# All of PSUM in one tile: bank pairs for the scores of two engines, single banks for the rest, and 74 score blocks on VectorE

## The chip, the cores and the metric

The kernel runs on one core of one Trainium2 chip. The metric is the device time of one execution in microseconds (us), as the median of several runs. The profile is one further execution, recorded by the hardware; PE is TensorE, DVE VectorE, ACT ScalarE, POOL GpSimd, SP SyncE.

## The reference, cut to what matters

A token sequence of 2048 x 448 goes two ways, and a gate per token mixes the results. Way A is softmax attention with 16 heads of 28 columns and an output projection. Way B is a two-dimensional real FFT, a product with a filter, and the way back.

```python
g = sigmoid((x * gate_w).sum(-1, keepdims=True))
q, k, v = (x @ wqkv).reshape(B, S, 3, 16, 28)...
p = softmax(einsum("bhqd,bhkd->bhqk", q, k) * 28 ** -0.5)
a = einsum("bhqk,bhkd->bhqd", p, v) @ wo
y = irfft2(rfft2(B_x) * (w_r + 1j * w_i))
out = g * a + (1 - g) * y
```

Here x is the input A_x.

## The kernel before

**Attention.** The heads stand in four groups of four (index g), the queries in four columns of 512 (index c): 16 pairs (g, c), which `plan_steps` numbers n = 0 to 15. For each n there are 16 key tiles of 128 (index kt), so 256 blocks (n, kt) of four heads. A score matmul takes the 32 rows of one head (28 columns, padding, and two rows that carry norms) against 512 queries, so it fills one of four row tiles of PE, and four matmuls of four different heads can stand side by side.

The exponential is made by two engines. `ND` says how many key tiles of each n go to VectorE; the rest go to ScalarE.

- ScalarE: a step is two heads of one block. PE writes two score matmuls into the two banks of `psA` or `psB`, which alternate; one `activation` of 1024 columns (line 1034) writes two slots of `ring`. The two steps of a block take heads 0 and 1, then heads 2 and 3.
- VectorE: for each of the four heads of a block PE writes one score matmul into a single bank (`bgi`), and a `tensor_scalar` of 512 columns (line 993, "the clamp") adds a bias, clamps at zero and writes the result as a 16-bit integer whose bits are a bfloat16: a piecewise linear power of two. GpSimd makes three further copies with shifted phase by `int64_add` (line 1003). So a block on VectorE has four versions of its probabilities, and each is multiplied with its own version of V (`vd`).

The product with V takes four column tiles (four heads) at a time and adds up in one bank of its own, `pv`: one set of four matmuls for a ScalarE block, four sets for a VectorE block. At the end of each n, `normalise` evacuates `pv`, and a chain of small transfers and two VectorE operations scales the result into `q`.

**Everything else.** `proj_group`, `w_block`, `v_block` and `x_block` make Q, K and V from x; `background` makes the FFT as matmuls with constant matrices in stages (`fwd`, `fwd2`, `mid`, `inv`); `out_tile` and `last_tile` add the output projection and the inverse transform for each 128 tokens. Each such product is an `Item` that occupies one single bank, of three (`bgt`), from its first matmul until VectorE or ScalarE has evacuated it.

**The order.** Every operation is registered with `Sched.op`, with the item whose bank it takes (`acq`) and the one that it gives back (`free`). Nothing decides at run time: `TABLE` holds two packed lists, the order in which all operations are issued and the bank of each item in the order of registration. `run` unpacks them and emits the operations; codes from `FILL0` up are groups of dummy matmuls on zeros into `pv`. The engines run their parts in that order and wait for one another by semaphores.

Of the kernel before, what the change touches and what calls it, by code (L numbers as in the profile page):

```python
# [15 lines left out]
F32 = mybir.dt.float32  # L16
U16 = mybir.dt.uint16
# [21 lines left out]
    "eNoN1mNjWEsUQNHxnMG5SW2ltm3bNtPUtm3btm3bto3UdvveX9hf1jakJbHEkXCCJDqJQWKSWCQ2iUPikngkPiEkAUlIEpHEJAkJI0lJMpKc"  # L39
    "UJKCZCApSU6SiniSmuQijHQlQAKiCScZSRoiSXaSlkQlitQk6Ugmkp7UILVINZKNZCG5SVUSheQhWUkOUodkJiVJKRKNlCa1SV5SloSQUFKO"  # L40
    "1Cf5SH5SgBQiBUkxUp6UIRVJYVKEFCXFySZSgWwmlUgJ0oq0JVvIVrKStCPbyHayiqwmVcgOsoZMJGtJZTKJTCZTyFSyjqwnG0g3YpVXG8l0"
    "MoPMJLOIU7PJHDKX7CTziCDzySy/gCwkcWk8Gp8uIovJDL+ELCUJaEK6jKDaRRLRnqQxWU5WkECFqMQ0Ck1Co9JoNDqNQcNoTBqLxqZx6G6y"
    "h+wl+0ioak6iqqfkGXlOXpCXJILcIQ3IfhJJ7pID5B55RV6TKOo+eUMekI7kIXlEHpNo6iCJrqaRGKouOUSS0mQ0pupEYqnkNAU9TJ6Qt2SD"
    "j63ekfckjvpA4qp4qhc5Qo6SlDS+akGOkan0I/lEptHPpAlJoBKq6fQLSaS+Qip6nCRWJ0hqmkR9gxk0TH0lp8hpkoau8WnpGXKWJFX1SG9y"
    "jpwnF8hMepEkU61JOnqJXCZXyFVyjSRX18kNcpOkULfIbZKeplRlaAaakZ4kmWhinoSnUj+hLE2t0qhYvByNzcvTXxCNz/XpVFpVgX6H6Dy9"
    "oqYiHUQyqIzqG0nGm5HvJAaPyX+Qn6Qp+UUyqT+QWf2DSjSLyqo6k+okDk/OK9OGpArtSDvRuDwhX+ezqc60C82uEvD1PhEP439IUp5D/SX/"
    "CKGUMrrac9qV5lSCSqqoprkU0Kw0G81Oc9DcKif9TXLR3NRQS/PQPCovzUdTcEfzKk/z05keaUDj83wqhBagmWlBWogWpkVofpWFhtJ4vCgt"
    "RtuTNqQ47U4LqIw8E+9BS9Ke1PJCyhhtHC+oCqv0vIjiJgMvTaUppoqqtLy4siYlr0p70RKqGi2pqtNSKh0vrVJzYXrTUlSZYaSMKkHT8Bq0"
    "Jk3FmSmrsvFyipi/UF5l5dn5SFpB5eGjaEU1mlZSeXkOPobWopVVB/IbqqiqKhcfS535AdVUTg6mNq2ucvMaqh7tQurTBjQfr0NrKm9qqc+u"
    "MC/DG9J4Bk1dWlsV4XVUDNOI1FUFeEJTkNdTCUwjmpnXV1l4WV6IJzHFeQlegefnFXkDFcs0VDFNXFOTN1KNVWNandfg8U0TVZQnMk1VMhOY"  # L50
    "YryZim1K8lo8jglXIaa5qsRb08o8mklpWqgIVY6X5m1oW9qOtlItVXnenjbjrVUqE86/uaimB2mjEpsmtK1KbkJNO1WVN6XNeQQPM9X4F9de"
    "NeFNeQeV0Xx3P9xP98t1VN1oJ1WX1+MZTDjtoprT7qSz+u0iaBTzx1XhLWhX1ZK2591UJlOKd1cduPQ9lPLpTHrTU/VSrWhtXoeDN9763iqN"
    "6aNa8+imr3I+tRlMve+n0po2vL8aQtE34o35ABX4gSqFSWoym0FqKB1GB6shqi3/6xrwf244JZ76+rwdH6oa8qKG+WGqI2/FC5jhqqDpxkeo"
    "fIb7Qkb4kWqU6sU78eKmO89jSpjRKovpzceoljyr6UvGqh68Jw/xXXkLXsaE+qG8GR2n8prxqjOP7xP4YTyhH8wnqES+iBnC4/i4PrGfqPrQ"
    "SWqyym860C58iipsipmpKokP81F9NN+HT1PZTHRf2cTw09UMNVP15aVNH5LT9KWzVAqf0s9Wa30qH9PH8rF9at+PpvFlzRy1kKb1i+hiOosu"
    "oXPVUprOD+fzVDkzgvfn5c18NYYvUHfoXXqPrqD36QO6ki5UI+gq+pA+oo/pE7qarqFP6SI1lq+l6+h6uoEO4BvpM7pYae/5JjqOL1HP6Qu6"
    "mb6kkXQ8f0WXqtd0C91Kt9FBdDtdpsbT5WoCXaFWquV0IK9kNvoddBwdSEuZQTypX6WS+Yl0El2tZvI1ajKdzquZmmatGs1n8XVqvZrEa5iS"
    "pqLZoPrxyXwG36jm8lF8Np9CJ/A5fCTfpPrTWmYi36yqmwF0Hp/Ct6gKpoqparapZXyrmk13qCW8tgk3c+g0nstsV03MPLpTNTUr+HKewyzl"
    "u1Qzs1vN5xFmj1rE1/LspoVZyTfyxXw+3ac6mTw+r9+rxpCFPJ9fx/P7TfyAmkv3qwK+oG9r2pmD6pA6rPbwOqa1mcqbm728kD+idvBMfifP"
    "7LP4oyqr38wHkGPqFF1AT9Mz9Cw9R7P54+o8vUCz+xz+Ir1EL9MTajW/Qrfwq3QVv0av0xv0pKprbtJTah9fw7uaBby/6WNu0dv0jFrPT6vc"  # L60
    "Zj9vY97QKL6zOad20rNqF91N99DzagPfS/fR/fQAPUgP0QtqFz9Md/Mj9Cg9Ri+q43QZPUFP8kuqgzlJT/GO5hzfzi+ro/wYv6KuqlZmG+9h"
    "eprz/Dg/wa+pLia9v64y+BvqMK9nuptDPLk/wluam+qWus/7mduqgq/oe5mG5gG/o7byC/wir+Qr+7uqij/IQ3goz+jbmwO8kbmnBphu5r6q"
    "6h+om7yaf6j6mt7mPb3C39K7fKCpbx6pW/yxOs3P8idqmhllnqqrfDi5xO/xZ2qcGW/e0RfquXrCL/OyfqIp55/ya3y0eakiVRPfwLxSTf0Y"
    "81rd5s38ZPNGhfs7/AV/q5r7l/ydivAzTDFf3JfwJX0p38K/V/PNB9WflPaRfJB5xT+qT2q2iefL+Bv8DL/OJ5np5rP6ogabIeQRf8af88J+"
    "gvmqvqnH/Av/yhubsaaIf8inmO/qh+JMsE/8p/qlPvOpRjLFNBtK3vJ3/D3/rf6omWaO+av+8n98sVloiP7AP/J/SorlZpYhYoihWgmm+5Hh"
    "huvXfK5ZYRaZN/w3L+qFpuIPlzqnz+V/8G+8oVda6wXmO8/th5lGfpmJKn5y0L+40UvMPPM/SMLqbn6p8drpaMIK1N39SpOE9fA9fS8PLLro"
    "7QO9yYSxpGyECdGhOoZIxvr47aaxj6qFiKKTMycOmW2Gieg6mtYiVHgRQ4OIIraY3SamiCVi6h1mp6nuY+lAxNYJxFGTUMTRIWK/SSJQ1PBx"
    "dZjYZ/aYeDq+TqDjiaEmvqjla/s6vq6v51eZ1SaRSCzq+7giqWjgy/uEerOZ7deYRHqUH+3H+LE+sR7nx/sJfq+ZQE6aOT6JDtNpxFbT0ifV"
    "yXRynVa08W19O9/exxEXTAff0Y80KXRKvc7U9J38QdPKf6Cp9Ef6iaYTqXUanVwcM+nFZ5pWp9OpRGyRXp8xJ8xh84WmFhl0Rl1I7DKFRV/f"
    "z6cQ030ykUmfNwdMZp1FZ9U5RUqRS3T2XXwGsdYcN9l0PnHKZNcD/EA/yGcU+cVgP8Tn0Dl1EXHEFBWnTSaRS2cVQ/1Zk1vHYHl0NnHOxGTD"  # L70
    "fD6dV180XX1mEYtlEbFZft3f3zIFdEEdh2UXf+h685fmEHlEIb3BFNYlxT9aStwx5UURTVgFQVleUVQ/N7lFaXHJFNNTfHE91d8zZcRDU0KX"
    "1DXEffPAlNI1RWldQBQU70w8VkaXFa19OXHbxGfFxHBfVidgI3xCVk1UFIlYdVFOV9Dl9RNTQnyjE/1I/9J8pxV1FVFJ/6A/aRU9yVfWTQVj"
    "03xV8Ys+Mq9NNV1c1Bdf6TNTVTcQv+ld89hU1zV0LVFbTPZPTU0dwmrpSiLSGNZMWPbFvDDzfG093y/wdfRCX1fU0+lZBpaRZWJ1tWOhLAqL"
    "yj6YuOyjWeQvm/o6GsvMGosGuol4axrphnoEaShasEainqgsWrJWrDVrwxKztqwda8+ysSO+sc7OOrAlfqPJwXKyXOyKaaKb6twsD8vLOrJO"
# [184 lines left out]
class Item:  # L259
    def __init__(self):  # L260
        self.bank = None
# [1209 lines left out]
```

## Time and profile before

| | |
|---|---|
| device time, median of 3 runs | 381.05 us (381.0 to 381.06) |
| device time of the profiled execution | 380.98 us |
| its span, first to last instruction | 379.2 us |
| busy time of PE | 371.3 us |
| busy time of ScalarE | 351.1 us |
| busy time of VectorE | 339.1 us |
| busy time of GpSimd | 234.4 us |
| granted clock of PE | 1.00 |

The profile page names for each group of instructions the line, the engine, the operation, the tiles written and read, the shape, the count, the busy time of the group, the mean duration of one, and the idle time of the engine ahead of them with its releaser. Almost all matmuls stand on line 432, the helper `mm`, so groups are told apart by their tiles: `psA` and `psB` are score pairs, `bg<-q,k` the scores for VectorE, `pvb` the products with V (from `ring` or from `pd`), other `bg` the remaining products. A matmul's recorded duration is longer than the time that it holds the engine up, since matmuls overlap; distances between starts say more. The timeline has one line for a run of like instructions: start, duration, engine, line, operation, tiles, shape, count. A row of the view by stretches gives the stretch, its length, then for each engine the busy time with the number of instructions, then the granted clock, the share of the DMA engines and the rate.

### The profile page before, as it was taken

Reading aid. Unit: us, or ns where it says so; the run is one execution under the profiler, and the core shown is the slowest. Engines: PE = TensorE matmul, PEld = TensorE weight load, DVE = VectorE, ACT = ScalarE, POOL = GpSimd, SP = SyncE. Lnnn points to the kernel's source line nnn. Section 1 sums busy time; section 2 is a strip of 40 time slices with the busy share of each in tenths; the row PEclk is TensorE's granted clock in tenths of the full one; section 3 lists DMA queues with packets and bytes.
Section 4 is the critical chain, followed back from the end, with each engine's and each line's share of the span. In section 5 each row is a group of like instructions: output and inputs, shape, how many; then the busy total and the mean of one; then the engine's idle time right before and its main releaser. Section 6 shows DMA issues by size and latency. Waiting matters only on the chain.

```text
span 379.2 us, 12643 instructions
## 1 busy us (share of the span) xinstructions
PE 371.3 (98%) x5117; PEld 142.4 (38%) x5117; DVE 339.1 (89%) x665; ACT 351.1 (93%) x389; POOL 234.4 (62%) x264
## 2 busy tenths in 40 slices
PE   8999999999999999999999999999999999999996
PEld 6634223342433333234333434233333323433564
DVE  1768899999999999999999999999999999988744
ACT  2799999999999999999999999999999999999841
POOL 4446465866778866565553565778597778483510
PEclk9999999999999999999999999999999999999999
DMA  6511101010210112211322212223222122222132
GB/s 145 157 34 44 29 18 36 4 36 2 41 52 22 44 41 54 55 38 30 68 60 93 69 40 49 57 61 70 45 64 74 30 69 72 86 64 72 35 103 75
DMA packets 31158, 21.23 MB, mean 56 GB/s; under 512 B 16260, under 2 KB 29052, under 8 KB 31100
## 3 DMA queue, kind: packets, MB, share of 16 engines
q1 hardware_dynamic: 29708, 19.96, 20.7%
q8 instruction: 40, 0.66, 0.7%
q10 hardware_dynamic: 1392, 0.46, 0.5%
q14 instruction: 18, 0.15, 0.1%
HBM read 14.51 MB, written 1.96 MB: 43 GB/s over the span
## 4 chain that ended last, share of the span: by engine, by line
PE 55%; ACT 31%; issue 6%; DVE 4%; DMA 2%; POOL 1%; SPq 0%; DVEq 0%; ACTq 0%; POOLq 0%
ACT ring L1034 31%; PE bg L432 24%; PE pvb L432 17%; PE psA L432 7%; PE psB L432 6%; DVE pd L993 2%; PE bg L435 1%; DMA CS<-cCS 1%; DVE X L1419 1%; POOL pd L1003 1%; DMA Wg<-in_B_w_i_dram 0%; DVE X L1298 0%; DVE q L1178 0%; DVE t L1362 0%; DVE wpq L1224 0%
## 5 line engine op out<-in xcount | busy, mean ns | idle before, releaser
L1003 POOL INT64_ADD pd<-pd x207 | 211.9, 1038 | 96.7 <-DVE pd L993 27.4
L1034 ACT ACTIVATE ring<-psA 128x1024 bf16<-128x1024 f32 x187 | 201.7, 1078 | 4.7 <-PE psA L432 3.2
L1034 ACT ACTIVATE ring<-psB 128x1024 bf16<-128x1024 f32 x187 | 201.7, 1079 | 2.6 <-PE psA L432 1.4
L993 DVE TENSOR_SCALAR pd<-bg 128x512 uint16<-128x512 f32 x276 | 180.9, 681 | 8.5 <-PE bg L432 3.5
L432 PE MATMUL pvb<-pd,vd 128*32 128x512 bf16 x1104 | 96.9, 384 | 0.1
L432 PE MATMUL bg<-q,k 32*128 32x512 bf16 x276 | 96.3, 383 | 0.2
L432 PEld LDWEIGHTS <-k 32*128 32x128 bf16 x1024 | 40.1, 91 | 122.4 <-issue 117.7
L432 PE MATMUL psB<-q,k 32*128 32x512 bf16 x374 | 73.2, 383 | 1.3 <-ACT ring L1034 0.7
L432 PE MATMUL psA<-q,k 32*128 32x512 bf16 x374 | 72.8, 383 | 0.5 <-ACT ring L1034 0.2
L432 PE MATMUL pvb<-ring,vw 128*32 128x512 bf16 x748 | 67.9, 384 | 0.0
L432 PEld LDWEIGHTS <-vd 128*32 128x32 bf16 x1104 | 25.3, 94 | 35.5 <-issue 31.1
L432 PEld LDWEIGHTS <-vw 128*32 128x32 bf16 x748 | 17.5, 94 | 22.7 <-issue 20.5
L432 PEld LDWEIGHTS <-xT 128*128 128x128 bf16 (+5 forms) x512 | 20.3, 97 | 10.7 <-issue 9.7
L432 PE MATMUL bg<-xT,wpq 128*32 128x512 bf16 (+3 forms) x244 | 21.2, 383 | 0.1
L1362 DVE TENSOR_TENSOR t<-bg,Wg 128x450 bf16<-128x450 f32 x32 | 18.8, 614 | 0.6 <-DMA Wg<-in_B_w_i_dram 0.4
L432 PE MATMUL bg<-xT,wpk 128*32 128x512 bf16 (+2 forms) x240 | 18.9, 383 | 0.0
L432 PE MATMUL bg<-wvr,xT 128*128 128x112 bf16 (+2 forms) x192 | 13.7, 213 | 0.0
L1178 DVE TENSOR_TENSOR q<-pvs,Rb 128x512 bf16<-128x512 f32 x15 | 10.9, 729 | 2.6 <-DMA Rb<-rsc 2.6
L1298 DVE TENSOR_TENSOR X<-bg,oc 128x226 bf16<-128x226 f32 (+1 forms) x32 | 12.3, 386 | 0.5
L432 PEld LDWEIGHTS <-CS 128*32 128x32 bf16 x384 | 9.0, 95 | 9.9 <-issue 5.6
L432 PE MATMUL bg<-xtok,CS 128*32 128x225 bf16 (+1 forms) x192 | 11.2, 294 | 0.7 <-DMA CS<-cCS 0.7
L742 DVE TENSOR_SCALAR k<-bg 128x512 bf16<-128x512 f32 x15 | 10.3, 685 | 1.3 <-PE bg L432 1.1
(117 smaller groups left out, 315.4 us busy)
## 6 DMA issues: line engine op xcount, KB each, us to landing
Rb<-rsc SPq DMA_DIRECT2D x60, 64.0 KB
CS<-cCS SPq DMA_DIRECT2D x16, 192.0 KB
V<-xtok SPq DMA_DIRECT2D x16, 113.0 KB
Wg<-in_B_w_i_dram SPq DMA_DIRECT2D x64, 28.1 KB
xtok<-Ab SPq DMA_DIRECT2D x16, 112.5 KB
xtok<-in_A_x_dram SPq DMA_DIRECT2D x3, 448.0 KB
Wg<-in_B_w_r_dram SPq DMA_DIRECT2D x32, 28.1 KB
out_dram<-wpq SPq DMA_DIRECT2D x6, 112.0 KB
```

What stands on the lines that cost most here:

```text
L432: self.pin(self.nc.tensor.matmul(out, lhsT=lhsT, rhs=rhs, start=start, stop=stop, **kw))
L435: self.pin(self.nc.tensor.transpose(out=out, in_=in_, identity=self.c("ident")[0:n, 0:n]))
L742: self.pin(nc.vector.tensor_scalar(out=dst, in0=self.bgi(it), scalar1=SQ, scalar2=None, op0=ALU.mult))
L993: self.pin(nc.vector.tensor_scalar(out=ys[:, s, :].bitcast(U16), in0=self.bgi(it), scalar1=127 * UNITS, scalar2=0.0, op0=ALU.add, op1=ALU. ...
L1003: self.pin(nc.gpsimd.int64_add(out=fl(pds), in0=fl(ys), in1=PHASE[f] * 0x0001000100010001))
L1034: self.pin(nc.scalar.activation(out=self.ring[:, u0:u0 + len(st), :], in_=slot[:, 0:len(st), :], func=ACT.Exp, scale=LN2 / UNITS))
L1178: e = self.dve(dv(512), lambda: self.pin(nc.vector.tensor_tensor(out=dst, in0=pvs[:], in1=self.Rb[:], op=ALU.mult)), ds, kk, lk=True)
L1298: self.pin(nc.vector.tensor_tensor(out=free_dims(self.X1[:, t, :], [[F, 2], [-1 if dif else 1, n]], (F - 1) * dif), in0=free_dims(self.bgi ...
L1362: self.pin(nc.vector.tensor_tensor(out=out[:], in0=self.bgi(it)[:, 0:F2].rearrange("p (a f) -> p a f", a=2), in1=free_dims(Wg[:], [[F, 2], ...
L1419: self.pin(nc.vector.tensor_tensor(out=free_dims(self.zt[0:FN], [[128, 4], [1, 128]], 512 * t), in0=self.bgi(it)[0:FN, :].rearrange("p (a ...
```

## The change

PSUM becomes one tile of eight banks, `banks`. Bank 7 is `pv`. An item gets a mask of bank kinds: 15 for a single bank, 7 for a pair (`slot`, two neighbouring banks). ScalarE's steps and VectorE's blocks both take pairs: a block has two operations on PE of two heads each, and two clamps of 1024 columns, in place of four of each with 512. All other products take single banks. The steps no longer have a fixed slot or a wait for the exponential two steps before; they acquire and free a pair like any item. `ND` goes from a sum of 69 to 74. The order and the banks are new lists; the old order holds six groups of dummy matmuls, the new one none. In the prologue and in `last_tile` the fixed homes in `psA` and `psB` become items. `kr[0] += self.ktr` adds a wait to the later reuse of `k[0]`.

```diff
 class Item:
-    def __init__(self):
-        self.bank = None
+    def __init__(self, mask=15):
+        self.bank, self.mask = None, mask
...
-    ND = [2,4,5,5]+[5,5,4,4]+[4,4,5,5]+[5,5,4,3]
+    ND = [3,5,5,5]+[5,5,4,4]+[4,4,5,5]+[5,5,5,5]
...
-        self.psA = ps.tile([P, 2, 512], F32, name="psA")
-        self.psB = ps.tile([P, 2, 512], F32, name="psB")
-        self.pv = ps.tile([P, 512], F32, name="pvb")
-        self.bgt = [ps.tile([P, 512], F32, name=f"bg{i}") for i in range(3)]
+        self.banks = ps.tile([P, 8, 512], F32, name="psA")
+        self.pv = self.banks[:, 7, :]
...
+    def slot(self, item):
+        return self.banks[:, item.bank:item.bank + 2, :]
+
     def bgi(self, item, dt=F32):
-        t = self.bgt[item.bank][:]
+        t = self.banks[:, item.bank, :]
...
-            for s in range(4):
-                it = Item()
-
-                def fm(s=s, g=g, c=c, kt=kt, it=it):
-                    self.mm(self.bgi(it), self.k[g][32 * s:32 * s + 32, 128 * kt:128 * kt + 128],
-                            self.q[g][32 * s:32 * s + 32, 512 * c:512 * c + 512], True, True, tile_position=(32 * s, 0))
+            for h in (0, 2):
+                it = Item(7)
+
+                def fm(h=h, g=g, c=c, kt=kt, it=it):
+                    for s in (h, h + 1):
+                        self.mm(self.slot(it)[:, s - h, :], self.k[g][32 * s:32 * s + 32, 128 * kt:128 * kt + 128],
+                                self.q[g][32 * s:32 * s + 32, 512 * c:512 * c + 512], True, True, tile_position=(32 * s, 0))
...
-                    self.pin(nc.vector.tensor_scalar(out=ys[:, s, :].bitcast(U16), in0=self.bgi(it),
+                    self.pin(nc.vector.tensor_scalar(out=ys[:, h:h + 2, :].bitcast(U16), in0=self.slot(it),
                                                      scalar1=127 * UNITS, scalar2=0.0, op0=ALU.add, op1=ALU.max))
-                p1s.append(self.dve(dv(512), f1, [m], due, free=it, name="dp1"))
+                p1s.append(self.dve(dv(1024), f1, [m], due, free=it, name="dp1"))
...
-            slot = self.psA if i % 2 == 0 else self.psB
-            deps = [exps[i - 2]] if i >= 2 else []
+            it, deps = Item(7), []
...
-            m = sc.op("PE", 0.23, fm, deps, -1000 + i * .001, 0.0, "row", name="score")
+            m = sc.op("PE", 0.23, fm, deps, -1000 + i * .001, 0.0, "row", it, name="score")
...
-            e = self.act(0.052 + 512 * len(st) / 1200.0, fe, [m] + exps[-1:], i * .001, name="exp")
+            e = self.act(0.052 + 512 * len(st) / 1200.0, fe, [m] + exps[-1:], i * .001, free=it, name="exp")
...
+        kr[0] += self.ktr
```

More of the change, by code (lines that the diff above doesn't have):

```diff
@@ L557, in prologue @@
                            (warm,), K0 + i * .01, dur=0.175, acq=None if i else hw, free=hw if i == 19 else None)
-        h3 = Item()
-        homes = [lambda: self.pv[:], lambda: self.psA[:, 0, :], lambda: self.psB[:, 0, :], lambda: self.bgi(h3)]
+        hi = [None, Item(), Item(), Item()]
+        homes = [lambda: self.pv[:]] + [lambda h=h: self.bgi(h) for h in hi[1:]]
         trs, self.xev = [], {}
@@ L584, in prologue @@
             b1 = (lambda i1=i1: self.bgi(i1)) if wi else (lambda: self.pv[:])
-            b2 = (self.psB if wi else self.psA)[:, 0, :]
+            i2 = Item()
+            b2 = lambda i2=i2: self.bgi(i2)
             first = {}
@@ L805, in w_block @@
             users.append(ops[-1])
+        else:
+            self.ktr = ops
         def fe():
@@ L1232, in last_tile @@
         i = t - 12
-        it = Item() if i > 1 else None
-        bank = lambda: (self.psA[:, 0, :] if i == 0 else self.psB[:, 0, :] if i == 1 else self.bgi(it))[:, 0:D]
-        ops = [self.lastexp[i]] if i < 2 else []
+        it = Item()
+        bank = lambda: self.bgi(it)[:, 0:D]
+        ops = []
         for k in range(8):
```

185 lines of the change are left out of this document (90 added, 95 removed).

## The prediction

> **What bounds the kernel now.** I read the page first: its line of engines, and the costliest groups.
>
> ```profile
> PE 371.3 (98%) x5117; PEld 142.4 (38%) x5117; DVE 339.1 (89%) x665; ACT 351.1 (93%) x389; POOL 234.4 (62%) x264
> ...
> L1003 POOL INT64_ADD pd<-pd x207 | 211.9, 1038 | 96.7 <-DVE pd L993 27.4
> L1034 ACT ACTIVATE ring<-psA 128x1024 bf16<-128x1024 f32 x187 | 201.7, 1078 | 4.7 <-PE psA L432 3.2
> L1034 ACT ACTIVATE ring<-psB 128x1024 bf16<-128x1024 f32 x187 | 201.7, 1079 | 2.6 <-PE psA L432 1.4
> L993 DVE TENSOR_SCALAR pd<-bg 128x512 uint16<-128x512 f32 x276 | 180.9, 681 | 8.5 <-PE bg L432 3.5
> ```
>
> No engine is idle enough to be ignored. ScalarE runs 187 + 187 = 374 exponentials, VectorE 276 clamps. The 276 clamps are 69 blocks of four heads; 16 x 16 = 256 blocks in all leave 187 blocks, at two steps each, to ScalarE: the 374. Next, the timeline of ScalarE: when its stream begins, its pace, when it ends.
>
> ```profile
> 12.74 1.02 ACT L1034 ACTIVATE ring<-psA 128x1024 bf16<-128x1024 f32 x1 [0.31 <-PE psB L432]
> ...
> 152.03 1.06 ACT L1034 ACTIVATE ring<-psA 128x1024 bf16<-128x1024 f32 x1
> 152.94 1.07 ACT L1034 ACTIVATE ring<-psB 128x1024 bf16<-128x1024 f32 x1
> ...
> 364.96 1.02 ACT L1034 ACTIVATE ring<-psB 128x1024 bf16<-128x1024 f32 x1
> ```
>
> Instructions overlap by some 0.1 us, so the distance of two starts is what one costs: 152.94 - 152.03 = 0.91 us. From the first start to the last there are 373 distances in 364.96 - 12.74 = 352.2 us, 0.944 each. At 0.905 they would take 337.6: ScalarE is within 15 us of its own floor, and those 15 us are waits. Then the busy time by stretches (PE, PEld, DVE, ACT, POOL, each with its count, in this order):
>
> ```profile
> 40.00:60.00 20.00, 20.00 (x248) 5.60 (x247) 18.21 (x33) 20.00 (x23) 13.06 (x15) 1.00 0.07 19
> ...
> 140.00:200.00 60.00, 59.83 (x870) 21.44 (x862) 58.27 (x115) 57.33 (x64) 34.46 (x36) 1.00 0.20 49
> 200.00:300.00 100.00, 98.58 (x1278) 34.94 (x1271) 97.93 (x206) 99.97 (x111) 67.98 (x70) 1.00 0.25 60
> ...
> 340.00:366.00 26.00, 26.00 (x482) 11.89 (x486) 17.39 (x28) 22.84 (x25) 10.63 (x11) 1.00 0.26 75
> 366.00:379.20 13.20, 9.67 (x244) 7.02 (x236) 6.80 (x12) 1.55 (x2) 0.00 (x0) 0.99 0.22 72
> ```
>
> From 200 to 300 ScalarE is full (99.97 of 100) with VectorE close behind (97.9). From 140 to 200 and from 340 to 366 it has gaps (57.3 of 60, 22.8 of 26) while PE has none (59.8, 26.0): there PE sets the pace. After 366 only PE has much left. So two engines take turns, and an edit that relieves ScalarE alone is worth less than its own sum.
>
> A busy PE is not a PE at its peak, so its timeline has to say what its work costs.
>
> ```profile
> 149.62 0.39 PE L432 MATMUL psA<-q,k 32*128 32x512 bf16 x2
> 149.63 0.39 PE L432 MATMUL bg<-q,k 32*128 32x512 bf16 x1
> 149.95 0.37 PE L432 MATMUL bg<-X,A 128*32 128x450 bf16 x4
> 150.15 0.39 PE L432 MATMUL pvb<-pd,vd 128*32 128x512 bf16 x4
> 150.47 0.39 PE L432 MATMUL psB<-q,k 32*128 32x512 bf16 x2
> ...
> 151.84 0.61 PE L432 MATMUL pvb<-pd,vd 128*32 128x512 bf16 x8
> 152.38 0.39 PE L432 MATMUL psB<-q,k 32*128 32x512 bf16 x2
> ```
>
> One set of four column tiles and the change to row tiles takes 150.47 - 150.15 = 0.32; two sets and the change 152.38 - 151.84 = 0.54. So a set is **0.22 us** and a change of tiling **0.10**. A row visit (two score matmuls and one matmul of a VectorE block side by side) takes 149.95 - 149.62 = 0.33 with its change back, so **0.43 us** with both changes. Every ScalarE step needs such a visit.
>
> **The change, part by part.**
>
> *Blocks.* ND sums to 74 instead of 69: 182 blocks, 364 steps. ScalarE loses 10 x 0.905 = **9.0 us** at its pace: two steps each in groups 0, 1 and 14, four in group 15. The groups between keep their number.
>
> *PE.* First the row visits, by the busy time of PE's instructions on tile k, which are the scores, the block matmuls and four small transposes:
>
> ```profile
> 0.00:379.20 379.20, 148.55 (x1028) 1.00 0.22 56
> ```
>
> 148.55 us at 0.39 a visit make 381 visits' worth, though there are 374 steps: some of the 276 single matmuls came alone or behind a score on the same rows. Now two heads of a block are one operation beside a step for the other two heads, four matmuls on four row tiles. If all 148 pairs ride so, 364 visits are left: 17 x 0.43 = -7.3 us. The visit with three matmuls (0.33) shows room for a guest at no price; four at once are in none of the rows quoted. Bounds: none rides, 148 x 0.22 = +32.6; all ride, 0. I take all, because steps alternate between the two halves of the heads, so that a partner is never more than one step away; one pair in four not riding would be +8. Against it, each block given to VectorE has four products with V instead of one: 5 x 3 = 15 more sets, 15 x 0.22 = +3.3. The six groups of dummy matmuls in the old order are not in the new one: 0 to -1.3. **PE: -7.3 + 3.3 - 1 = -5.0 us.**
>
> *VectorE.* 276 clamps of 512 become 148 of 1024.
>
> ```profile
> 151.32 0.68 DVE L993 TENSOR_SCALAR pd<-bg 128x512 uint16<-128x512 f32 x1
> 151.92 0.38 DVE L1294 COPY oc<-bg 128x226 f32<-128x226 f32 x1
> 152.22 0.68 DVE L993 TENSOR_SCALAR pd<-bg 128x512 uint16<-128x512 f32 x1
> ```
>
> Start to start, 512 columns cost 0.60 and 226 cost 0.30: 0.30 / 286 = 1.05 ns a column, some 0.06 fixed. 1024 columns: 0.60 + 0.54 = 1.14 (from 1.07 with no fixed part to 1.20 with no gain). Before 276 x 0.60 = 165.6, after 148 x 1.14 = **168.7** (158 to 178). VectorE gets 3 us more, but lies better: the middle groups, whose blocks stay, save 0.12 a block, and the five new blocks go to the ends, where it has gaps (17.4 of 26 from 340). I cost it at nothing; the cover is those gaps. In the stretch 200 to 300 only 2 us are left, so a wider clamp of 1.20 would cost it nothing either, but a late one would show.
>
> The Trainium skill, in "VectorE: DVE Perf Modes", section "The TRN2 errata", prices a PSUM read at 120 cycles plus the columns at 0.96 GHz: 0.66 and 1.19 us, so by that page VectorE would go from 182 to 176. The distance of starts above shows half of that fixed part, and the row decides.
>
> *GpSimd.* 15 more copies by 1.04 = 15.6 us on an engine with 97 us of idle time in its group; hidden.
>
> *Banks.* Scores had two pairs to themselves; single matmuls and all other products shared three banks. Now bank 7 holds the products with V, and the bank list of the new table (687 numbers) gives all 364 steps and 148 block pairs banks 0-1, 2-3 or 4-5, and 124 of the 175 other items bank 6; the others lie mostly at the start and the end. Two new waits follow. A score can wait for a clamp that holds its pair, with everything on PE behind it, and ScalarE runs dry one exponential (0.9 us) later. And a product for bank 6 can wait for the evacuation of the one before. I cost both at 0 (an order written out can place other work there), between 0 and the rival below.
>
> *Start.* The four transposes of the prologue change banks, with the same instructions: 0, within half a microsecond.
>
> **The sum.** ScalarE allows -9.0, PE -5.0; PE has no gap in the stretches above and the tail is its leftover work:
>
> ```profile
> 366.11 0.39 PE L432 MATMUL pvb<-ring,vw 128*32 128x512 bf16 x4
> ...
> 375.28 0.39 PE L432 MATMUL bg<-wpk,q 128*32 128x448 bf16 x4
> ```
>
> The last exponential's product is at 366.11 and PE still works until 375.7. If ScalarE ends 9 us sooner and PE is only 5 us ahead, the other 4 reappear in this tail. So the smaller saving counts: span 379.2 - 5.0 = 374.2; what lies around the span was 380.98 - 379.2 = 1.8; **376.0 us**. The profiled execution (380.98) stands at the median (381.05).
>
> **The rivals.**
>
> *ScalarE's whole gain.* For it: the 100 us in which it is full, and its waits for PE are short in total:
>
> ```profile
> ACT ring L1034 <- PE psA L432: 4.5, 8, 0.8
> ```
>
> If PE's background can be shifted into its slack, 9.0 us come off: 372.0, and 370 with some of the waits. The Trainium skill's first page, "Trainium Kernel Development and Optimization", section "Performance Expectations", says that matmul busy time is a bad measure of the distance to the roofline; read so, the 98% prove no bound and this rival stands. The gaps of ScalarE in the stretches where PE has none speak against: 18%.
>
> *The pairs do not ride.* A quarter alone costs 8 us of PE, a seventh eats the whole 5.0 (21 x 0.22 = 4.6): then PE gives nothing, and the time stays between 379 and 381.8. Against it: the alternation of halves. 15%.
>
> *Bank 6 becomes the bound: slower.* An item holds its bank from its first matmul until its evacuation ends:
>
> ```profile
> 186.71 0.39 PE L432 MATMUL bg<-xT,wpq 128*32 128x512 bf16 x4
> ...
> 188.44 0.62 PE L432 MATMUL bg<-xT,wpq 96*32 96x512 bf16 x8
> ...
> 189.22 0.68 DVE L742 TENSOR_SCALAR q<-bg 128x512 bf16<-128x512 f32 x1
> ```
>
> This projection took 189.90 - 186.71 = 3.2 us, because visits and products lay between its four sets; its bare parts are 4 x 0.22, some 0.35 until VectorE starts, 0.68: 1.9. 124 items follow each other in bank 6 in about 354 us (12 to 366). It decides from a mean hold of 354 / 124 = 2.85 us: at 1.9 they take 236 us and nothing shows; at 2.9 they take 360, 6 us more than the old stretch, and the span grows with it: 385 to 387. Against it: many items are shorter than a projection. The Trainium skill, in "PSUM — Partial Sum Buffer", section "PSUM bank collisions raise a hardware error", lets no two engines work in one bank's quadrant at a time and advises another bank for reading while matmuls run; by it the next write cannot overlap the evacuation, which is what makes the holds add. No row here shows a bank reused at once. A late clamp that holds up a score belongs to the same side. 22%.
>
> **How the numbers follow.** Forecast, 373.5 to 378.8: 45%. Whole gain, below 373.5: 18%. Nothing gained, 378.8 to 381.8: 15%, about half of it faster by more than 0.2%. Slower: 22%, half of it above 384.5. A measurement of this kernel can tell about 0.2% (0.8 us) from no change. So faster 0.70, same 0.08, slower 0.22. The range, 370.0 to 384.5, leaves out the worst half of the slow cases and the best of the whole gain.
>
> **What would show it.** Clamps of 1024 columns 1.14 us apart (1.07 to 1.20). Row visits of four matmuls still 0.33 long, and the busy time on tile k near 364 x 0.39 = 142 us; much above says that pairs came alone. The last exponential near 357, and a tail after it longer than the 13.2 us of now; were the tail as long as now, the whole gain came. A wait of PE for VectorE on background products, with ScalarE's gaps in the middle groups grown, says bank 6. The forecast is wrong if PE's work falls by more than I count, or if its gaps, few now, become many.

## The result, and the profile after

| | before | after |
|---|---|---|
| device time, median (6 runs of each) | 380.79 us | 383.58 us (382.41 to 384.31) |
| profiled execution, its span | 380.98, 379.2 us | 382.41, 380.5 us |
| ratio, 95% interval | | 1.0072 [1.0059, 1.0085] |

The change makes the kernel slower by 0.7% (2.2 to 3.2 us). The forecast was 376.0, the range 370.0 to 384.5. The profiled execution after is the fastest of its six, so the two profiles show 1.4 of the 2.8 us. Medians and ratios, here and below, leave out executions in a slower state, which are two of c4's five (387.8 and 388.7 us) and one of d1's eleven (608.4 us).

The engines' line of the page after, and its chain of waits by engine:

```profile
PE 372.4 (98%) x5152; PEld 145.8 (38%) x5153; DVE 338.1 (89%) x536; ACT 345.7 (91%) x379; POOL 249.1 (65%) x279
...
PE 78%; DVE 12%; ACT 5%; issue 2%; POOL 1%; DMA 1%; ACTq 0%; DVEq 0%; POOLq 0%
```

ScalarE lost 5.4 us of busy time, VectorE 1.0, PE gained 1.1. The chain before was:

```profile
PE 55%; ACT 31%; issue 6%; DVE 4%; DMA 2%; POOL 1%; SPq 0%; DVEq 0%; ACTq 0%; POOLq 0%
```

ScalarE's share went to the two others. The groups of the two engines that empty the pairs:

```profile
L1033 ACT ACTIVATE ring<-psA 128x1024 bf16<-128x1024 f32 x364 | 340.3, 1048 | 17.3 <-PE psA L425 16.3
...
L993 DVE TENSOR_SCALAR pd<-psA 128x1024 uint16<-128x1024 f32 x148 | 180.2, 1220 | 16.4 <-PE psA L425 14.7
```

ScalarE waits 16.3 us for scores now. Before it was 4.5 + 2.5 = 7.0, since the scores of its two pairs stand in two rows of the view of waits:

```profile
ACT ring L1034 <- PE psA L432: 4.5, 8, 0.8
...
ACT ring L1034 <- PE psB L432: 2.5, 6, 0.6
```

Where it waits, the windows say. Their borders are the first exponentials of the groups n = 0, 5 and 11 and the last one; first the kernel before, then the one after:

```profile
12.70:122.50 109.80, 109.11 (x1449) 39.97 (x1447) 100.41 (x198) 108.91 (x123) 71.18 (x87) 1.00 0.13 31
122.50:254.90 132.40, 131.39 (x1812) 46.76 (x1804) 129.17 (x259) 129.70 (x144) 81.45 (x83) 1.00 0.22 54
254.90:365.00 110.10, 108.60 (x1541) 40.36 (x1537) 99.03 (x189) 106.67 (x117) 75.33 (x75) 1.00 0.25 64
365.00:379.20 14.20, 10.67 (x264) 7.53 (x252) 7.11 (x12) 2.53 (x4) 0.00 (x0) 0.99 0.25 83
```

```profile
14.10:133.60 119.50, 117.56 (x1676) 46.59 (x1672) 115.90 (x190) 108.22 (x120) 80.64 (x97) 1.00 0.10 27
133.60:268.30 134.70, 134.22 (x1827) 50.69 (x1819) 133.53 (x240) 130.47 (x144) 83.15 (x86) 1.00 0.28 74
268.30:369.80 101.50, 101.37 (x1386) 35.23 (x1386) 79.23 (x89) 101.00 (x110) 76.92 (x75) 1.00 0.14 44
369.80:380.50 10.70, 7.09 (x176) 4.87 (x164) 3.74 (x7) 2.61 (x4) 0.00 (x0) 0.97 0.17 55
```

The columns are the stretch, its length, then busy time and count of PE, weight loads, VectorE, ScalarE and GpSimd. Groups 0 to 4 became 9.7 us longer, 5 to 10 by 2.3; 11 to 15 became 8.6 shorter and the tail 3.5. VectorE stood at 91% in the first stretch and now at 97%, ScalarE went there from 99 to 91%. In the last stretch it is the other way: VectorE fell from 90 to 78%, ScalarE is full (101.00 of 101.50). Background work moved forward, out of the last groups and the tail: of VectorE's operations other than clamps, 24 more start in the stretch of the groups 0 to 4, 32 more in that of 5 to 10, and 61 fewer after it. PE is full up to the last exponential, before and after, so the longer first stretch is PE's own: by distances of starts it spends 4.3 us more there on other products, 3.5 more on products with V and 1.7 more on scores. How VectorE looks where it is full, its timeline of the kernel after shows:

```profile
143.05 1.22 DVE L993 TENSOR_SCALAR pd<-psA 128x1024 uint16<-128x1024 f32 x1
144.19 0.62 DVE L1315 CAST Ab<-psA 128x450 bf16<-128x450 f32 x1
144.84 1.23 DVE L993 TENSOR_SCALAR pd<-psA 128x1024 uint16<-128x1024 f32 x1
```

Each instruction starts before the last one's recorded end; a clamp holds the engine up for 144.19 - 143.05 = 1.14 us.

### The profile page after: what moved, and what is told of

It reads as the page before. It is cut to its first block, busy times and chain, and to the rows that moved or that the text cites. A ratio compares the mean times of both kernels' runs of the same rounds, so it can differ in the third digit from the quotient of the medians.

```text
span 380.5 us, 12661 instructions
## 1 busy us (share of the span) xinstructions
PE 372.4 (98%) x5152; PEld 145.8 (38%) x5153; DVE 338.1 (89%) x536; ACT 345.7 (91%) x379; POOL 249.1 (65%) x279
## 4 chain that ended last, share of the span: by engine, by line
PE 78%; DVE 12%; ACT 5%; issue 2%; POOL 1%; DMA 1%; ACTq 0%; DVEq 0%; POOLq 0%
PE psA L425 77%; DVE pd L993 5%; ACT ring L1033 4%; PE psA L428 1%; DVE X L1298 1%; POOL pd L1003 1%; DMA CS<-cCS 1%; DVE sq L744 1%; DVE k L739 1%; DVE oc L1294 1%; DVE Ab L1315 1%; DVE pvs L1166 0%; DVE nrow L761 0%; DVE q L739 0%; DVE q L1178 0%
## 5 line engine op out<-in xcount | busy, mean ns | idle before, releaser
L1033 ACT ACTIVATE ring<-psA 128x1024 bf16<-128x1024 f32 x364 | 340.3, 1048 | 17.3 <-PE psA L425 16.3
L1003 POOL INT64_ADD pd<-pd x222 | 227.5, 1040 | 105.8 <-PE psA L425 30.0
L993 DVE TENSOR_SCALAR pd<-psA 128x1024 uint16<-128x1024 f32 x148 | 180.2, 1220 | 16.4 <-PE psA L425 14.7
L425 PE MATMUL psA<-q,k 32*128 32x512 bf16 x1024 | 147.4, 382 | 1.5 <-ACT ring L1033 0.8
L425 PE MATMUL psA<-pd,vd 128*32 128x512 bf16 x1184 | 104.7, 384 | 0.3 <-POOL pd L1003 0.2
L425 PE MATMUL psA<-ring,vw 128*32 128x512 bf16 x728 | 67.5, 383 | 0.0
L425 PE MATMUL psA<-xT,wpq 128*32 128x512 bf16 (+4 forms) x248 | 20.3, 382 | 0.3
L425 PE MATMUL psA<-xT,wpk 128*32 128x512 bf16 (+3 forms) x247 | 19.7, 382 | 0.1
L1362 DVE TENSOR_TENSOR t<-psA,Wg 128x450 bf16<-128x450 f32 x32 | 18.5, 615 | 0.0
L1298 DVE TENSOR_TENSOR X<-psA,oc 128x226 bf16<-128x226 f32 (+1 forms) x32 | 12.4, 391 | 1.0
L425 PE MATMUL psA<-wvr,xT 128*128 128x112 bf16 (+2 forms) x192 | 12.8, 213 | 0.1
```

Of the source, the lines that this page charges most:

```text
L425: self.pin(self.nc.tensor.matmul(out, lhsT=lhsT, rhs=rhs, start=start, stop=stop, **kw))
L993: self.pin(nc.vector.tensor_scalar(out=ys[:, h:h + 2, :].bitcast(U16), in0=self.slot(it), scalar1=127 * UNITS, scalar2=0.0, op0=ALU.add, o ...
L1003: self.pin(nc.gpsimd.int64_add(out=fl(pds), in0=fl(ys), in1=PHASE[f] * 0x0001000100010001))
L1033: self.pin(nc.scalar.activation(out=self.ring[:, u0:u0 + len(st), :], in_=self.slot(it)[:, 0:len(st), :], func=ACT.Exp, scale=LN2 / UNITS))
L1298: self.pin(nc.vector.tensor_tensor(out=free_dims(self.X1[:, t, :], [[F, 2], [-1 if dif else 1, n]], (F - 1) * dif), in0=free_dims(self.bgi ...
L1362: self.pin(nc.vector.tensor_tensor(out=out[:], in0=self.bgi(it)[:, 0:F2].rearrange("p (a f) -> p a f", a=2), in1=free_dims(Wg[:], [[F, 2], ...
```

## The experiments

Kernels are compared by the ratio of their time to that of the kernel before, measured beside them. "Against the changed kernel" is (ratio - 1.0072) x 380.8 us, good to about 0.8 us; the changed kernel's own ratio, 1.0072, was measured once, beside the result, and not again beside these runs. The expectations name the differences of medians instead (-3.0, -0.4, -1.6 for the first three cuts); by ratios these are -3.4, -0.6 and -2.1.

### One engine's work cut at a time

**a1**: the scores of the blocks on VectorE are left out, and the clamps read a constant in SBUF.

```diff
-                    for s in (h, h + 1):
+                    for s in ():
...
-                    self.pin(nc.vector.tensor_scalar(out=ys[:, h:h + 2, :].bitcast(U16), in0=self.slot(it),
+                    self.pin(nc.vector.tensor_scalar(out=free_dims(ys[:, h, :].bitcast(U16), [[128, 8], [1, 128]]),
+                                                     in0=free_dims(self.cst[:].bitcast(F32), [[0, 8], [2, 128]]),
```

> The changed kernel (383.6 us) without the 296 score matmuls of VectorE's blocks: PE does not touch their bank pairs, and the 148 clamps read a table of constants in SBUF, 1024 columns as before, so VectorE keeps its load but no pair is ever held by a clamp, and no clamp waits for PE. Theory A (PE waits at the shared pairs for clamps and for the visits of two pairs one after the other): 5 to 9 us less, PE's row visits back at 0.32 us each and ScalarE's idle time, 17 us, more than halved. Theory B (ScalarE is again the only bound): within 1 us. Theory C (VectorE, or bank 6 behind it, is the bound): within 2 us, since VectorE's work and all of bank 6 stay.

Measured: 414.09, 1.0856 [1.0813, 1.0899]. It misfired. The cores' view gives a granted clock of 0.946 (after: 0.999). The row of the clock (tenths of full speed in 40 slices of the span) and two groups show two things that were not meant to change:

```profile
PEclk9888579999999999699999999998999998699999
```

```profile
L1004 POOL INT64_ADD pd<-pd x222 | 271.1, 1235 | 86.2 <-PE psA L425 18.4 <-DVE pd L993 16.3 <-DVE sq L744 16.1
L993 DVE TENSOR_SCALAR pd<-cst 128x1024 uint16<-128x1024 f32 x148 | 148.4, 1009 | 13.3 <-PE psA L425 13.3
```

PE's clock sank in places, and GpSimd's additions took 1235 ns instead of 1040 beside clamps that read SBUF. It tells nothing about the scores. The runs that follow change lengths, counts and order, and leave every operand in its memory.

**a2, a3, a4**: products with V on 448 of 512 columns; exponentials on 992 of 1024; clamps on 960 of 1024.

```diff
-                        self.mm(self.pv[32 * s:32 * s + 32, :], lw, rhs, cnt[0] == 1, cnt[0] == cnt[1],
+                        self.mm(self.pv[32 * s:32 * s + 32, 0:448], lw, rhs[:, 0:448], cnt[0] == 1, cnt[0] == cnt[1],
...
-            def fe(st=st, it=it, u0=u0):
+            def fe(st=st, it=it, u0=u0, w=512 if i < 14 else 496):
...
-                def f1(h=h, it=it, ys=ys):
+                def f1(h=h, it=it, ys=ys, w=512 if di < 9 else 480):
```

Each w is then the column bound of input and output.

> The changed kernel with the products with V cut from 512 to 448 columns (64 queries of each block left out): 478 sets, each 64 x 0.43 = 27 ns shorter, 13 us less work on PE and nothing else changed. Theory A (PE's work and its waits add up to the time): 8 to 13 us less. B (ScalarE): 0 to 2 us less. C (VectorE or bank 6): 0 to 4 us less.

> The changed kernel with the exponentials from the fifteenth step on cut from 1024 to 992 columns: 350 x 28 ns = 9.9 us less work on ScalarE and nothing else changed. A (PE): 0 to 3 us less. B (ScalarE): 8 to 10 us less. C: 0 to 2 us less.

> The changed kernel with the clamps from the tenth block on cut from 1024 to 960 columns: 130 x 67 ns = 8.7 us less work on VectorE, and each pair given back 67 ns sooner. A (PE, with its waits for clamps among the waits): 1 to 3 us less. B (ScalarE): 0. C (VectorE or bank 6 behind it): 5 to 9 us less.

| | cut | median | ratio | against the changed kernel |
|---|---|---|---|---|
| a2, PE | 12.8 us | 380.61 | 0.9984 [0.9969, 0.9999] | -3.4 |
| a3, ScalarE | 9.3 us | 383.2 | 1.0057 [1.0037, 1.0077] | -0.6 |
| a4, VectorE | 8.7 us | 381.94 | 1.0018 [1.0000, 1.0035] | -2.1 |

(a3 is 350 x 0.0265; its expectation took 9.9.) No engine alone binds: none of the cuts gives more than about a quarter of itself. ScalarE, whose 9 us the forecast counted on, gives nothing that stands clear of the 0.8 us.

### Which pairs stand side by side on PE

Two heads of a block are a pair on two of the four row tiles. A visit is a run of score matmuls between two products of the other tiling; the pairs in it are neighbours. From the order and the starts of all 1024 score matmuls: 139 of the 148 VectorE pairs stand beside a step, but at 56 places two neighbours are for the same two heads, and so for the same row tiles. PE's timeline of the changed kernel, around 92 us:

```profile
89.35 0.42 PE L425 MATMUL psA<-q,k 32*128 32x512 bf16 x4
...
90.47 0.39 PE L425 MATMUL psA<-q,k 32*128 32x512 bf16 x2
...
91.31 0.51 PE L425 MATMUL psA<-q,k 32*128 32x512 bf16 x4
...
93.24 0.60 PE L425 MATMUL psA<-q,k 32*128 32x512 bf16 x4
```

A pair alone takes 0.39 from the first start to the last end. At 89.35 a pair rides along for 0.03; at 93.24 both pairs are heads 2 and 3, and the second starts 0.226 later. At 91.31 they are different heads, but the second pair's banks came free 0.08 us late, with the end of a clamp. b1 turns the order of the halves round in 45 blocks of ScalarE and 10 of VectorE, which leaves 5 of the 56 places; b2 turns so that there are 107; b3 does to the kernel before what b1 does (24 places to 17, any two matmuls of one visit counted, neighbours or not).

```diff
-                for s in range(4):
+                for s in (2, 3, 0, 1) if (n, kt) in FLIP_A else range(4):
...
-            for h in (0, 2):
+            for h in (2, 0) if (n, kt) in FLIP_D else (0, 2):
```

> The changed kernel, with order, banks, instructions and shapes kept, but another choice of which two heads come first in 45 ScalarE blocks and 10 VectorE blocks, so that neighbours in a row visit take different row tiles. In the changed kernel 55 of the 148 pairs stand next to a step of the same two heads and run after it, 0.22 us each in its trace; here 5 do. Theory D (these collisions ate PE's saving, and PE is the bound): 51 x 0.22 = 11 us less work on PE, time 5 to 11 us below the changed kernel's 383.6, so 372.5 to 378.6. Theory E (PE's sets only move up against the waits at bank pairs, and VectorE sets the pace): 0 to 3 us below.

> The opposite: 17 ScalarE blocks and 12 VectorE blocks turned so that the neighbours on the same row tiles go from 56 to 107, all else kept. D: 51 x 0.22 = 11 us more work on PE, 6 to 11 us above the changed kernel. E: 0 to 3 us above.

> The kernel before with the heads of 16 ScalarE blocks and 14 VectorE blocks in another sequence, so that matmuls which meet on a row tile within a visit go from 24 to 17, all else kept. D: 7 x 0.22 = 1.5 us less, between 0.5 and 1.5. E: within 0.5 us.

| | median | ratio | against |
|---|---|---|---|
| b1 | 382.56 | 1.0050 [1.0031, 1.0070] | -0.8, the changed kernel |
| b2 | 389.29 | 1.0225 [1.0209, 1.0242] | +5.8, the changed kernel |
| b3 | 381.51 | 1.0013 [1.0001, 1.0025] | +0.5, the kernel before |

Busy time on tile k (the windows over the whole span): before, after, b1, b2:

```profile
sum 379.20, PE 148.55; mean PE 148.55
```

```profile
sum 380.50, PE 147.93; mean PE 147.93
```

```profile
sum 381.40, PE 143.53; mean PE 143.53
```

```profile
sum 386.90, PE 154.81; mean PE 154.81
```

51 places x 0.226 = 11.5 us of PE's time were freed in b1, and tile k fell by 4.4. The same stretch of b1 shows what took the rest:

```profile
88.80 0.50 PE L427 MATMUL psA<-q,k 32*128 32x512 bf16 x4
...
90.70 0.43 PE L427 MATMUL psA<-q,k 32*128 32x512 bf16 x4
...
92.67 0.51 PE L427 MATMUL psA<-q,k 32*128 32x512 bf16 x4
...
96.25 0.49 PE L427 MATMUL psA<-q,k 32*128 32x512 bf16 x4
```

No visit is 0.60 long any more, but now the second pair waits almost everywhere. Over the run the second pair of a visit waits for a clamp at 51 places, 9.6 us (27 places, 4.0 us in the changed kernel), and for an exponential at 29, 3.8 us (10, 1.9 us). In the kernel before these were 8 and 21 places, 1.4 and 3.6 us: already the change itself turned waits for ScalarE into waits for VectorE. The collisions were real, and half of their doubling in b2 reaches the end (5.8 of 51 x 0.226 = 11.5 us); but in the changed kernel most of their time only fills a wait for a pair that VectorE or ScalarE still holds.

### Two and three engines at once

c1 makes each clamp as two of 512 columns on the same pair, which adds VectorE work; c2, c3 and c4 join the edits of a2 and a4, of a2 and a3, and of all three.

```diff
-                    self.pin(nc.vector.tensor_scalar(out=ys[:, h:h + 2, :].bitcast(U16), in0=self.slot(it),
-                                                     scalar1=127 * UNITS, scalar2=0.0, op0=ALU.add, op1=ALU.max))
+                    for e in range(2):
+                        self.pin(nc.vector.tensor_scalar(out=ys[:, h + e, :].bitcast(U16), in0=self.slot(it)[:, e, :],
+                                                         scalar1=127 * UNITS, scalar2=0.0, op0=ALU.add, op1=ALU.max))
```

> The changed kernel, each clamp of 1024 columns made as two of 512 on the same pair, in the same place. VectorE gets 148 x (2 x 0.60 - 1.14) = 8.9 us more work and each pair of a block is held 0.06 us longer; PE and ScalarE have the same work. Theory 'PE and VectorE bound it in turns' (VectorE is 96 to 100% full in the groups 1 to 10, which hold 97 of the 148 clamps): 383.6 + about 5 (4 to 8), that is 387.5 to 391.5. Rival 'VectorE follows, bank 6 or the pairs bind through the waits of PE': a pair held 0.06 longer 97 times costs a wait at most where the score waits (27 of them): 383.6 to 385.5.

> The changed kernel with both cuts of before at once: products with V on 448 of 512 columns (-12.8 us of PE) and clamps on 960 of 1024 columns from the tenth block on (-8.7 us of VectorE); 64 queries, and in the clamped blocks 32 of 512 columns of the scores, are left out. Alone they gave -3.0 and -1.6. Theory 'PE and VectorE in turns': each cover goes with the other, so together clearly more than the sum: -7 to -11, 372.5 to 376.5. Rival 'neither binds, bank 6 does': the sum or less, -4.6 or less, 379 to 381.

> The changed kernel with products with V on 448 columns (-12.8 us of PE) and exponentials on 992 columns (-9.9 us of ScalarE). Alone -3.0 and -0.4. Theory 'PE and VectorE in turns': ScalarE is no part of it in the groups 1 to 10, only in 11 to 15: -3.5 to -5, 378.5 to 380. Rival 'PE and ScalarE in turns', the picture of the forecast: -8 to -11, 372.5 to 375.5.

> The changed kernel with all three cuts: products with V on 448, exponentials on 992, clamps on 960 columns. Theory 'PE and VectorE in turns, ScalarE third': the three engines lose 2.3 to 3.5% of their work each, the time follows with about 2.3 to 2.8% (8.5 to 10.5 us): 373 to 375. Rival 'bank 6 binds', whose items keep their length: not below 379.

| | median | ratio | against the changed kernel | sum of the single cuts |
|---|---|---|---|---|
| c1, VectorE +8.9 | 386.95 | 1.0161 [1.0144, 1.0179] | +3.4 | |
| c2, PE and VectorE | 378.96 | 0.9952 [0.9935, 0.9970] | -4.6 | -5.5 |
| c3, PE and ScalarE | 378.30 | 0.9930 [0.9913, 0.9946] | -5.4 | -4.0 |
| c4, all three | 374.66 | 0.9839 [0.9818, 0.9861] | -8.9 | -6.1 |

c1 lies just below the theory's 4 and above the rival's 1.9. c2 is a miss for "PE and VectorE in turns": no more than the sum. c3 goes a little further than the theory's -5, and c4 lies within its 373 to 375. Only c3 and c4, which have ScalarE's cut in them, give more than the sum of the single cuts; c4 gives 2.3% for some 2.6 to 3.4% of each engine's busy time. The rival that bank 6 binds falls: c4 leaves its items as they were and goes to 374.7, below the 379 set for it.

### The same cuts on the kernel before

The edits of a4, a3 and a2 in the lines of the kernel before, for instance

```diff
-                    self.pin(nc.vector.tensor_scalar(out=ys[:, s, :].bitcast(U16), in0=self.bgi(it),
+                    self.pin(nc.vector.tensor_scalar(out=ys[:, s, 0:w].bitcast(U16), in0=self.bgi(it)[:, 0:w],
```

> The kernel before, with its clamps on 480 of 512 columns from the tenth block on (60 blocks x 4 x 0.031 = -7.5 us of VectorE; 32 of 512 columns of those blocks keep old values). In the changed kernel a like cut gave -1.6. Theory 'the change moved the bound to VectorE in the groups 0 to 10': before, VectorE was 73 and 86% full in the groups 0 and 1 and had gaps, so 0 to -0.5, 380.4 to 381. Rival 'the same loop of three engines in both, only with more waits at the pairs': -1.3 to -2, 379 to 379.7.

> The kernel before, with its exponentials on 992 of 1024 columns from the fifteenth step on (360 x 0.027 = -9.7 us of ScalarE; 16 of 512 columns of those scores keep old values). In the changed kernel the same cut gave -0.4. Theory 'the bound moved from PE and ScalarE to VectorE': ScalarE was a bound in some 150 of 380 us before (31% of the chain of waits, full from 200 to 300), so -1.5 to -3, 378 to 379.4. Rival 'the same loop in both': -0.4, about 380.5.

> The kernel before, with products with V on 448 of 512 columns (463 sets x 0.027 = -12.4 us of PE; 64 queries of each 512 are left out). In the changed kernel the same cut gave -3.0. Theory 'PE and ScalarE in turns before': -3 to -5 until ScalarE binds throughout, 376 to 378. Rival 'the same loop in both': -3.0, 377.9.

| cut of | kernel before | ratio, interval | changed kernel |
|---|---|---|---|
| VectorE | d1: -0.5 | 0.9988 [0.9978, 0.9999] | a4: -2.1 |
| ScalarE | d2: -1.5 | 0.9960 [0.9941, 0.9978] | a3: -0.6 |
| PE | d3: -2.1 | 0.9945 [0.9925, 0.9964] | a2: -3.4 |

VectorE and ScalarE change places, as the theory said, at the lower edge of its numbers for ScalarE and below it for PE. VectorE's cut is worth 1.6 us more after the change and PE's 1.3, both just clear of the noise; that ScalarE's is worth 0.9 less is within it. So the change did make VectorE a bound; that ScalarE is less of one is not shown by these cuts alone.

### Other orders

d4, e1 and e2 have the changed kernel's instructions; only the lists in `TABLE` are new.

From e1's:

```diff
 TABLE = (
-    "c6WhDER3MdxP/Vtrk1V248Z052WhHFiTTaaW5SG77MF78l48zMQ18UwFqAiFZBpZWFYCMjFNZajN6/AqUEQ6k0pWhWpQl9fjOWR1qAHRTFGZ"
...
+    "c6WhDER3MdxP/Vtrk1V248Z052WhHFiTWpaHbDK77MF78l48tgkzcU08UwEqQiGZRhaWlYBMZajN6/CYpgoUkc6kklWhGtTl9XgOWR1qQDRT"
...
 )
```

> The changed kernel with the same instructions in another order and with other banks (the written-out table alone is new): work is shifted by up to 60 places where a chain of waits over the whole order, set up with the shortest distances of starts in the trace of the changed kernel, became shorter. In that chain the changed kernel lay on VectorE for most of 24 to 270 and on ScalarE from 288 to 355. Theory 'the order puts too much of VectorE's work ahead of group 11, and that can be mended only in part by order, since the blocks stay in their groups': -2 to -4, 379.5 to 381.5. Rival 'three pairs shared by two engines cost it whatever the order': 383 or more.

> The changed kernel, the same instructions and banks; some 60 of 3392 places in the order moved behind 20 us (39 by more than four places: products with V of the groups 1 to 12 mostly, five products and scores of other kinds, two normalisations later, one clamp earlier), each where the longest chain of waits became shorter. This chain now counts the DMA queue of SP, the waits of GpSimd for VectorE and large transfers, which the order of d4 broke (GpSimd's copies came late and PE waited 17 us for them). Theory 'a good part of the loss is the order': -1 to -2.2, 381.4 to 382.6. Rival 'the work itself, wherever it stands': 383.3 to 384.

> As e1, with some 1600 places moved by more than three (90 at most, 5 on the mean) and some banks changed, behind 20 us. By the same chain 3.5 us shorter than the changed kernel. Theory 'a good part of the loss is the order': -1.5 to -3.5, 380 to 382. If it is far above e1, the order can't be changed widely without a measure of what GpSimd and the DMA queues bear.

Measured: d4 420.92, 1.1038 [1.1019, 1.1057]; e1 384.51, 1.0088 [1.0069, 1.0107]; e2 390.12, 1.0241 [1.0213, 1.0268]. d4 misfired. PE waited for GpSimd's copies, for which it waited 0.2 us in the changed kernel:

```profile
PE psA L425 <- POOL pd L1003: 17.4, 15, 2.5
```

and its first exponential came 5.7 us later than the changed kernel's. That is 23 of the 39 us between the two spans; the rest was not followed up (its granted clock was 0.974). e1 is the changed kernel within its interval (+0.6), though its longest chain should have been 2.2 shorter; e2 is worse by 6.4. The chain did not foretell the time in any of the three. Whether a better plan of this change exists is not settled by that: the order and the bank lists came with the change, no run separates them from it, and other numbers of blocks for each group were not tried.

### Where each engine binds

f1 cuts PE everywhere, ScalarE only in the groups 0 to 10 and VectorE only in 11 to 15: each of the two where the windows show it with room.

```diff
-            def fe(st=st, it=it, u0=u0):
+            def fe(st=st, it=it, u0=u0, w=496 if i >= 14 and st[0][0] < 11 else 512):
...
-                def f1(h=h, it=it, ys=ys):
+                def f1(h=h, it=it, ys=ys, w=480 if n > 10 else 512):
```

> The changed kernel with products with V on 448 columns everywhere (-12.8 us of PE), exponentials on 992 columns in the groups 0 to 10 alone (240 x 0.027 = -6.4 us of ScalarE) and clamps on 960 columns in the groups 11 to 15 alone (50 x 0.063 = -3.1 us of VectorE): 22.3 us of cuts, where all three everywhere had 31 and gave -8.3. Theory 'VectorE binds beside PE in the groups 0 to 10, ScalarE beside PE in 11 to 15': both small cuts lie where their engine doesn't bind, so no more than PE alone, -3 to -3.6, 380.1 to 380.8. Rival 'all three bind everywhere': in proportion, 22.3 / 31 x 8.3 = -6, 377.6 to 378.

Measured: 380.84, 1.0002 [0.9991, 1.0013], -2.7 against the changed kernel: PE's cut alone (a2, -3.4), and not the -6 of "all three everywhere". The 6.2 us between f1 and c4 come from the other halves of the two cuts, VectorE's in the groups 0 to 10 and ScalarE's in 11 to 15. The runs with two cuts say how it divides: PE with VectorE everywhere (c2) lies 1.9 us below f1, PE with ScalarE everywhere (c3) 2.7. That PE and VectorE bind up to group 10, PE and ScalarE from 11 on, fits all of these; the two binding halves joined to PE's cut, without the others, were not run.

## Why the prediction was wrong, point by point

**What bounds the kernel before** was right: PE and ScalarE, not VectorE (d3 -2.1, d2 -1.5, d1 -0.5).

**The row visits failed: -7.3 was -1.9.** The step was "I take all, because steps alternate between the two halves of the heads, so that a partner is never more than one step away". From the starts of the matmuls PE made 357 visits before (the sum took 381, from the busy time), in 124.9 us, and 327 after, in 126.0 (first start to the next product of the other tiling). With the 30 changes of tiling that fell away, 0.10 each, that is 1.1 - 3.0 = -1.9. At the forecast's 0.43 a visit it would have been -12.9, more than for the 17 visits counted, for only 9 pairs came alone and many visits hold two steps. But riding was not free. What the visits took beyond 0.33 each was 124.9 - 357 x 0.33 = 7.1 us before and 126.0 - 327 x 0.33 = 18.1 after: 11.0 more, where the sum had 0. A partner that is never more than one step away was often the wrong one: visits in which a row tile comes twice were 22 before and 59 after, and took 7.8 and 16.2 us of this. The other 2.5 are longer waits for banks.

Of the forecast's other terms of PE, the dummy matmuls gave the 1.0. Products with V, forecast at 3.3 more for 15 more sets, took 4.9 more, and all other products 5.1 less, by distances of starts, with the changes to row tiles inside these two figures; 33 of the other matmuls now stand ahead of the first score. In sum PE took 363.0 us before and 362.9 after, from the first score to the start of the last matmul: the -5.0 was -0.1. The first score came 1.3 us later, and so the span was 380.5 instead of 374.2.

**VectorE at nothing was the second failure**, and b1 shows that mending the collisions alone gives 0.8 us. The duration was right, 1.14 us from start to start, and the sum of VectorE's work stayed (busy 339.1 and 338.1). The cover was wrong: the blocks went to the ends, but background work moved from the last groups and the tail into the groups 0 to 10, and VectorE, at 97 and 99% in the first two stretches, became a bound beside PE there. The gaps at the end, which were to hide it, grew instead (78% busy). The Trainium skill, in "TensorEngine Tiling (Array Packing)", section "PSUM Bottleneck", warns that after tiling on PE the evacuation of PSUM may become the bottleneck. c1 agrees, where 8.9 us more of VectorE's work cost 3.4.

**The two new waits at 0.** The wait of a score for a clamp is the one that came: 27 second pairs instead of 8, and ScalarE dry for 16.3 us instead of 7.0. (The prediction read 4.5 for the latter; the row that it quotes holds the scores of `psA` alone, and `psB` has 2.5 more.) The other did not: by order and trace bank 6 held its 124 items for 2.56 us on the mean, under the forecast's 2.85, and c4 shows that it doesn't bind. The rival on the slower side (22%) named "a late clamp that holds up a score" as belonging to it; that half was right, the mechanism that it was built on was not.

**"The pairs do not ride" (15%)** was the rival closest to the trace: a quarter not riding was to cost 8 us, and riding at a price cost 11.0. Its end at 381.8 ("PE gives nothing, and the time stays") was too low, since it let nothing but PE's rows change.

**The start, 0 +- 0.5, failed too.** The first score waited in the changed kernel. K is ready at 10.85 + 0.69 = 11.54:

```profile
10.85 0.69 DVE L607 TENSOR_SCALAR k<-psA 128x512 bf16<-128x512 f32 x1
...
12.33 1.33 PE L428 MATMUL psA<-cst,xtok 128*128 128x128 bf16 x21
...
13.60 0.39 PE L425 MATMUL psA<-q,k 32*128 32x512 bf16 x2
```

Before, Q was ready at 12.21 and the score followed at once:

```profile
11.53 0.68 DVE L613 TENSOR_SCALAR q<-psB 128x512 bf16<-128x512 f32 x1
...
12.31 0.39 PE L432 MATMUL psA<-q,k 32*128 32x512 bf16 x2
```

So 0.10 us became 2.06, behind transposes of x that the kernel before makes later. It is no chance: the wait is 2.05 to 2.15 in every trace with the changed kernel's prologue except a1 (2.3) and d4, whose prologue is reordered too, and 0.10 in all five with the prologue of before. In the pair of profiles the first exponential is 1.3 us later (though Q and K were ready 0.7 sooner), what follows it takes 366.5 in both, and the span's whole difference is 1.3.

How much of these 2 us reaches the end was not tried: the transposes that fill them are work that PE need not do later. The other traces allow an estimate. In twelve profiled executions of the changed kernel and its variants (all but a1, c4 and d4, whose clock was lower) the first exponential starts between 13.9 and 18.3 us, in the five of the kernel before and its variants between 11.6 and 12.7. An execution that starts late ends late by about as much: a4's profile, at 18.3, is 3.4 us above a4's median, the changed kernel's, at 14.05, is 1.2 below. A straight line through each group (slopes 1.1 and 0.9) puts the start that belongs to the median at 14.9 and 12.4. By this estimate 2.4 of the 2.8 us lie ahead of the first exponential, about 2 of them in the wait of the first score, and what follows takes about as long as before. So the late start would be most of the loss, and the visits and VectorE the reason why no saving made up for it. That stays an estimate: with the old prologue in the changed kernel, which was not run, some transposes would come back behind the first score.

**ScalarE, -9.0.** The steps went away, but not as a bound: in the changed kernel it binds only from 268 on. The signs named for it read so: last exponential near 357, seen 369.8; tail longer than 13.2, seen 10.7; row visits of 142 us, seen 147.9 ("much above says that pairs came alone": 9 did; the others met the wrong partner). **GpSimd's** 15 us more stayed hidden (234.4 to 249.1 busy).

**PE as the bound.** The forecast let the time follow PE's saving to the full 5.0. In fact 12.8 us less of PE's work are worth 3.4. The Trainium skill, on its first page, "Trainium Kernel Development and Optimization", section "Performance Expectations", calls matmul busy time a bad measure of what is left; PE was 98% busy before and after, and the 3.4 agree with that.

## What to carry to other kernels

Where three engines stood within some ten per cent of one another, as here, a saving on one was worth a quarter of itself at best; ask stage by stage which engine has no room, for an engine with gaps on the mean can be full for two thirds of the run. That two matmuls can share PE needs not only a partner nearby but one on other row tiles whose banks are free at that moment; count the partners in the order, pair by pair. When a new order is made, look at when the first score can start, as well as at the stages. A cut of one engine's work by 2 to 3%, alone, in pairs and by stages, found the bound here, where busy shares and the chain of waits did not.

## What was not expected of the hardware

- Two score matmuls on the same row tile start 0.226 us apart; on different ones 0.006.
- GpSimd's additions took 1235 ns beside clamps that read SBUF, 1040 beside clamps that read PSUM (a1), although these clamps were shorter, 1009 ns against 1220. The Trainium skill, in "SBUF — State Buffer", section "SBUF: two separate sides", says that GpSimd and VectorE share a port to SBUF and can contend there; a1's slower additions fit that; no run shows that the port is the reason.
- The granted clock was 0.946 in a1 and 0.974 in d4, with PE busy 92 and 91% of the span, 0.965 in c4's profile with 97%, and 0.996 to 1.000 in all others, with 96 to 98%. What sets it was not tried.
- A bank was written again within 0.12 us of the end of its evacuation at 36 of the 123 changes of item in bank 6, and at none of them before that end.
